# A convolution and low-rank mixer kernel: hand-ordered groups of eight token tiles, tiled matmuls, and transposes by DMA

## The chip, the cores and the metric

The kernel runs on one core of a Trainium2 chip. The metric is device time in microseconds (us). A quoted time is the median of a kernel's runs; a quoted ratio is the mean time of one kernel's fast runs over the mean time of the other's fast runs in the same rounds, so it is not quite the ratio of the two medians.

Engines: PE is TensorE (matmul), PEld its weight loads, DVE is VectorE, ACT ScalarE, POOL GpSimd, SP SyncE. A "tile" of tokens here is 128 tokens; a row or column tile of PE is a part of its 128 by 128 array.

## The reference, cut to what matters

The batch is 8, the sequence 4224 tokens (33 tiles of 128), the model width 192. There are 8 heads of 24 channels and 7 taps; the rank is 32.

```python
# softmax over the 7 taps, then a causal convolution along the sequence, one filter a head
out = np.einsum('hk,bskhg->bshg', w, x_unf)        # -> x of the next part
# mixer
xt = x.transpose(0, 2, 1)
h = xt @ U @ V                                     # U: 4224 x 32, V: 32 x 4224
u = x + h.transpose(0, 2, 1)
ch = np.maximum(u @ w_ch1, 0.0) @ w_ch2            # 192 -> 768 -> 192
return u + ch
```

So there are two large products a token (W1, 192 to 768, and W2, 768 to 192), and a low-rank mix over all tokens of a batch, which needs the whole convolution of that batch first.

## The kernel before

A scheduler chooses the order. For each batch: a convolution as two 128 by 128 band matmuls a head, the product with U over 33 tiles, the product with V, then groups of 4 token tiles (8 groups of 4 and one group of 1), each with PE transposes, W1, ReLU and W2.

```python
for hh in range(H):                                   # conv, 504 or 288 columns
    nc.tensor.matmul(out=cps, lhsT=band_sb[:, hh, :], rhs=x_sb[:, 1+s0:1+s1, hc], start=True,  stop=False)
    nc.tensor.matmul(out=cps, lhsT=pband_sb[:, hh, :], rhs=x_sb[:, s0:s1, hc],    start=False, stop=True)
# ... cut: U and V products on the full array, 192 columns each
for t in range(gt):                                   # two transposes a token tile
    nc.tensor.transpose(out=trps[...], in_=u_sb[:, j, 0:P], identity=ident[:])
    nc.tensor.transpose(out=trps[...], in_=u_sb[:, j, D-P:D], identity=ident[:])
nc.vector.tensor_copy(out=uT_lo, in_=trps[...])       # and uT_hi on ACT
# ... cut: loops over the six 128-wide blocks m of W1, in threes
nc.tensor.matmul(out=h1ps, lhsT=W1_sb[:, m*P:(m+1)*P],   rhs=uT_lo, start=True,  stop=False)
nc.tensor.matmul(out=h1ps, lhsT=W1hp_sb[:, m*P:(m+1)*P], rhs=uT_hi, start=False, stop=True)   # 64 of its rows are zero
# ... cut: ReLU on ACT (two of three) and DVE (one of three), W2, add u, store
```

The width 192 does not fit 128 rows, so the second W1 matmul has 64 rows of zeros: a quarter of the W1 work is spent on them.

The softmax here doesn't subtract the row's maximum and nothing guards it: scores larger than these inputs give would overflow.

## Time and profile before

557.93 us when it was predicted (median of 3 runs).

| | before |
|---|---|
| PE, DVE, ACT busy | 86%, 52%, 45% |
| first W1 matmul starts | 62.3 us |
| PE waits for the band weights | 34.9 us |
| PE waits for the transposed u (uT_lo) | 16.0 us |
| a batch in the steady part | about 62 us |

The first page has these lines: busy time of each engine, then the span in 40 slices in tenths, with the granted PE clock under it.

```profile
PE 481.0 (86%) x3760; PEld 307.3 (55%) x3760; DVE 290.2 (52%) x625; ACT 250.2 (45%) x490; POOL 33.4 (6%) x72
...
PE   0226999999999999999999999999999999978886
...
PEclk9999899999999999999999999999999999989999
DMA  9930912247222921166112911194112011201212
```

PE is at nine tenths or more for nearly all of the span after a slow start, at full clock. The DMA engines are lightly used, save while x loads. The list of waits says what PE stood still for (us in total, times, longest):

```profile
PE cps L208 <- DVE band_sb L167: 34.9, 8, 17.0
PE h1ps L294 <- DVE uT_lo L280: 16.0, 29, 0.8
```

The timeline gives the paces. Here is one group of 4 token tiles on PE (start us, duration us, line, what, count):

```profile
204.06 0.59 PE L303 MATMUL h1ps<-uT_hi,W1hp_sb 128*128 128x512 bf16 x2
204.49 2.38 PE L329 MATMUL smps<-W_sb,rl_sb 128*128 128x192 bf16 x24
206.70 0.22 PE L268 MATMUL trps<-ident,u_sb 128*128 128x128 bf16 x1
206.76 0.22 PE L273 MATMUL trps<-ident,u_sb 128*128 128x128 bf16 x1
...
207.85 0.81 PE L294 MATMUL h1ps<-uT_lo,W_sb 128*128 128x512 bf16 x3 [0.33 <-DVE uT_lo L280]
```

The starts count, not the durations, since matmuls are pipelined: 24 W2 matmuls in 2.21 us (0.092 each), a transpose every 0.056 us, a W1 matmul every 0.215 us.

### The profile page before, as it was taken

How to read it: one execution, taken by the hardware profiler on the slowest of the kernel's cores; microseconds unless marked ns; L12 is line 12 of the kernel's file. 1: busy time of each engine (PE TensorE's matmuls, PEld its weight loads, DVE VectorE, ACT ScalarE, POOL GpSimd, SP SyncE). 2: the span in 40 equal slices, each digit the busy share in tenths (PEclk: the TensorE clock that was granted, in tenths of full speed). 3: DMA queues.
4: the chain of work that ended last, by engine and by line, in shares of the span. 5: the costliest groups of instructions: out<-in, count | busy, mean ns of one | idle time of the engine just before them, and what ended most of it. 6: DMA issues, size and time to landing. Idle time of an engine off the chain costs nothing. (4 is left out here: it accounts for less than half of the span.)

```text
span 558.3 us, 9274 instructions
## 1 busy us (share of the span) xinstructions
PE 481.0 (86%) x3760; PEld 307.3 (55%) x3760; DVE 290.2 (52%) x625; ACT 250.2 (45%) x490; POOL 33.4 (6%) x72
## 2 busy tenths in 40 slices
PE   0226999999999999999999999999999999978886
PEld 0003665666566656666566656665666666645554
DVE  2991754457444844466444844465444744464444
ACT  1113345544555445544554454545444545514443
POOL 9400100010000100010001000010000000000000
PEclk9999899999999999999999999999999999989999
DMA  9930912247222921166112911194112011201212
GB/s 122 159 36 0 117 58 66 75 70 113 77 67 64 117 86 59 58 98 111 58 58 65 146 58 57 58 127 84 58 58 65 28 59 60 78 13 51 64 58 64
DMA packets 75371, 40.69 MB, mean 73 GB/s; under 512 B 41312, under 2 KB 75296, under 8 KB 75296
## 3 DMA queue, kind: packets, MB, share of 16 engines
q0 software_dynamic: 39216, 14.11, 22.3%
q1 hardware_dynamic: 36112, 25.99, 14.8%
q8 instruction: 29, 0.48, 0.4%
q14 instruction: 14, 0.11, 0.1%
HBM read 28.24 MB, written 25.95 MB: 97 GB/s over the span
## 5 line engine op out<-in xcount | busy, mean ns | idle before, releaser
L313 ACT ACTIVATE rl_sb<-h1ps 128x512 bf16<-128x512 f32 (+1 forms) x288 | 152.4, 560 | 75.7 <-PE h1ps L303 68.3
L319 DVE TENSOR_SCALAR rl_sb<-h1ps 128x512 bf16<-128x512 f32 x144 | 92.9, 645 | 153.4 <-PE h1ps L303 71.6
L329 PE MATMUL smps<-W_sb,rl_sb 128*128 128x192 bf16 x1584 | 156.6, 246 | 3.1
L329 PEld LDWEIGHTS <-rl_sb 128*128 128x128 bf16 x1584 | 129.6, 98 | 34.7 <-ACT rl_sb L313 15.7
L222 ACT ACTIVATE y_sb<-cps 128x288 bf16<-128x288 f32 (+1 forms) x128 | 64.1, 501 | 188.4 <-PE cps L215 188.4
L294 PE MATMUL h1ps<-uT_lo,W_sb 128*128 128x512 bf16 (+1 forms) x432 | 123.2, 362 | 19.1 <-DVE uT_lo L280 16.0
L303 PE MATMUL h1ps<-uT_hi,W1hp_sb 128*128 128x512 bf16 (+1 forms) x432 | 124.3, 363 | 0.1
L338 DVE TENSOR_TENSOR out_sb<-smps,u_sb 128x384 f32<-128x384 f32 (+1 forms) x136 | 74.2, 545 | 61.1 <-PE smps L329 59.8
L208 PE MATMUL cps<-x_sb,band_sb 128*128 128x288 bf16 (+1 forms) x128 | 45.3, 354 | 43.3 <-DVE band_sb L167 34.9
L252 DVE TENSOR_TENSOR u_sb<-y_sb,smps 128x384 bf16<-128x384 bf16 (+1 forms) x136 | 68.4, 538 | 8.8 <-PE smps L245 6.2
L294 PEld LDWEIGHTS <-W_sb 128*128 128x128 bf16 x432 | 41.5, 97 | 50.7 <-issue 34.7
L303 PEld LDWEIGHTS <-W1hp_sb 128*128 128x128 bf16 x432 | 41.2, 97 | 46.6 <-issue 12.3
L281 ACT ACTIVATE uT_hi<-trps 128x512 bf16<-128x512 bf16 (+1 forms) x72 | 40.4, 560 | 37.7 <-DVE uT_lo L280 37.1
L215 PE MATMUL cps<-x_sb,pband_sb 128*128 128x288 bf16 (+1 forms) x128 | 45.4, 354 | 1.6 <-DVE pband_sb L185 1.6
L245 PE MATMUL smps<-tt_sb,V_sb 128*128 128x192 bf16 x264 | 43.8, 251 | 2.7 <-DVE u_sb L252 1.3
L268 PE MATMUL trps<-ident,u_sb 128*128 128x128 bf16 x264 | 45.2, 220 | 0.0
L273 PE MATMUL trps<-ident,u_sb 128*128 128x128 bf16 x264 | 45.2, 220 | 0.0
L208 PEld LDWEIGHTS <-band_sb 128*128 128x128 bf16 x128 | 12.6, 98 | 47.8 <-DVE band_sb L167 39.9
L245 PEld LDWEIGHTS <-V_sb 128*128 128x128 bf16 x264 | 25.1, 99 | 24.8 <-issue 7.7
L228 PE MATMUL tt_psum<-y_sb,U_sb 128*32 128x192 bf16 x264 | 30.9, 260 | 4.0 <-ACT y_sb L222 4.0
L273 PEld LDWEIGHTS <-u_sb 128*128 128x128 bf16 x264 | 26.0, 99 | 7.7 <-issue 0.3
L268 PEld LDWEIGHTS <-u_sb 128*128 128x128 bf16 x264 | 26.0, 99 | 6.9 <-issue 0.3
(68 smaller groups left out, 144.9 us busy)
## 6 DMA issues: line engine op xcount, KB each, us to landing
out_dram<-out_sb SPq DMA_DIRECT2D x128, 192.0 KB, 2.0
x_sb<-in_x_dram POOLq DMA_DIRECT2D x8, 1584.0 KB, 13.3
out_dram<-out_sb SPq DMA_DIRECT2D x8, 96.0 KB, 1.6
W_sb<-in_moe_w_ch_dram POOLq DMA_DIRECT2D x1, 288.0 KB, 10.8
U_sb<-in_moe_U_dram POOLq DMA_DIRECT2D x1, 264.0 KB, 14.5
V_sb<-in_moe_V_dram POOLq DMA_DIRECT2D x1, 264.0 KB, 13.5
W_sb<-in_moe_w_ch_dram POOLq DMA_DIRECT2D x1, 192.0 KB, 10.2
W1hp_sb<-in_moe_w_ch_dram POOLq DMA_DIRECT2D x1, 96.0 KB, 9.8
```

The lines of the kernel that those rows point to most:

```text
L208: nc.tensor.matmul(out=cps[:, 0:cb, :], lhsT=band_sb[:, hh, :], rhs=x_sb[:, 1 + s0 : 1 + s1, hc], start=True, stop=False,)
L222: nc.scalar.activation(out=y_sb[:, s0:s1, hc], in_=cps[:, 0:cb, :], func=ACT.Copy)
L245: nc.tensor.matmul(out=smps[:, t, :], lhsT=V_sb[:, j * P : (j + 1) * P], rhs=tt_sb[:], start=True, stop=True,)
L252: nc.vector.tensor_tensor(out=u_sb[:, j0 : j0 + n, :], in0=y_sb[:, j0 : j0 + n, :], in1=smps[:, 0:n, :], op=ALU.add,)
L268: nc.tensor.transpose(out=trps[:, t * P : (t + 1) * P], in_=u_sb[:, j, 0:P], identity=ident[:],)
L273: nc.tensor.transpose(out=trps[:, GT * P + t * P : GT * P + (t + 1) * P], in_=u_sb[:, j, D - P : D], identity=ident[:],)
L294: nc.tensor.matmul(out=h1ps[:, 0:ntok], lhsT=W1_sb[:, m * P : (m + 1) * P], rhs=uT_lo[:, 0:ntok], start=True, stop=False,)
L303: nc.tensor.matmul(out=h1ps[:, 0:ntok], lhsT=W1hp_sb[:, m * P : (m + 1) * P], rhs=uT_hi[:, 0:ntok], start=False, stop=True,)
L313: nc.scalar.activation(out=rl_sb[:, m, 0:ntok], in_=h1ps[:, 0:ntok], func=ACT.Relu,)
L319: nc.vector.tensor_scalar_max(out=rl_sb[:, m, 0:ntok], in0=h1ps[:, 0:ntok], scalar1=0.0)
L329: nc.tensor.matmul(out=chps[:, tt, :], lhsT=rl_sb[:, m, t * P : (t + 1) * P], rhs=W2_sb[:, m, :], start=(m == 0), stop=(m == MC - 1),)
L338: nc.vector.tensor_tensor(out=out_sb[:, 0:n, :], in0=chps[:, 0:n, :], in1=u_sb[:, j : j + n, :], op=ALU.add,)
```

## The change

The intent is to take work off PE and off the start:

- The token tiles of all batches form one row of 264 and are worked in 33 groups of 8, across batch borders, in an order written by hand. W2 of a group runs one group later than its W1.
- W1 has three chunks of 64 rows. The two halves of a group (4 token tiles each) lie on rows 0 to 63 and 64 to 127, so two matmuls of 64 rows can run side by side on two row tiles. No zero rows are left.
- Convolution runs on four 64 by 64 tiles, half the columns.
- The U products use four column tiles of 32, the V products four row tiles of 32. Two small matmuls a batch add up the four partial sums.
- u is transposed by the DMA engines (12 blocks of 128 by 128 a group) instead of PE.
- Band weights come from a strided read of a small DRAM tile instead of 120 DVE operations (so many are in the trace; the prediction says 112); x loads in three chunks.

```diff
-    GT = 4
+    GT = 8
+    NTT = B * NT
+    NG = NTT // GT
+    ctx.enter_context(tc.manual_schedule())
 ...
+    def conv(b, h, i0, i1, engs):
+        for halo in range(2):
+            for r in range(2):
+                for c in range(2):
+                    nc.tensor.matmul(
+                        out=pp[r][HB * c : HB * c + HB, 0 : nn[r] * GS],
+                        lhsT=band[HB * r : HB * r + HB, h, HB * halo : HB * halo + HB],
+                        rhs=xt[b][HB * r : HB * r + HB, st : st + 2 * nn[r] - 1 : 2, hc],
+                        start=(halo == 0), stop=(halo == 1),
+                        tile_position=(HB * r, HB * c),
+                    )
 ...
+            c = ttn[b] % 4                       # U products
+            nc.tensor.matmul(out=ttp[b][32 * c : 32 * c + 32, 0:D], lhsT=U_sb[:, j, :],
+                rhs=yt[b][:, j, :], ..., tile_position=(0, 32 * c))
 ...
+                nc.tensor.matmul(                # V products
+                    lhsT=V_sb[32 * q : 32 * q + 32, (j // 8) * 2 + j % 2, :],
+                    rhs=ttb[b][32 * q : 32 * q + 32, :], ..., tile_position=(32 * q, 0))
 ...
-                nc.tensor.transpose(...)
-            nc.vector.tensor_copy(out=uT_lo[:, 0:ntok], in_=trps[:, 0:ntok])
-            nc.scalar.activation(out=uT_hi[:, 0:ntok], ...)
+        nc.sync.dma_start_transpose(
+            out=uTt[g][:].rearrange("p i c t -> p (i c) t"),
+            in_=ut[g][:].rearrange("p i c f k -> p (i c f k)"))
 ...
+            for c in range(3):                   # W1
+                for hf in range(2):
+                    nc.tensor.matmul(out=pp[hf][:],
+                        lhsT=W1_sb[HB * hf : HB * hf + HB, c, m * P : (m + 1) * P],
+                        rhs=uTt[g][HB * hf : HB * hf + HB, :, c, :],
+                        start=(c == 0), stop=(c == 2), tile_position=(HB * hf, 0))
 ...
+    for g in range(NG + 1):
+        if g + 1 < NG:
+            h_group(g + 1)
+            transp(g + 1)
+        for b in loadq.get(g, []):               # x of a later batch, all chunks at once
+            x_tile(b)
+            for ch in XCH:
+                x_load(b, *ch)
+        if g < NG:
+            w1(g)
+        for b, h in convq.get(g, []):
+            conv(b, h, 0, NB1, "AA")
+        ...                                      # W2 of group g - 1, U products
```

## The prediction

> **What bounds it now.** PE, in order. The first page shows PE 86% busy, DVE 52%, ACT 45%. Start-up takes 62 us to the first W1 matmul; in it PE waits 34.9 us for the DVE that builds the bands (list of waits). After that PE is at nine tenths or more per slice, granted clock near 1.0. The timeline gives the paces: 512-column W1 matmuls start every 0.215 us, 192-column W2 matmuls every 0.092 us (24 in 2.21 us), transposes every 0.056, 504-column conv matmuls every 0.21, U and V products 0.083 to 0.1. Per batch (estimate): W1 21.3, W2 18.2, conv 5.4, U and V products 6.3, transposes 3.7: 55 us, against about 62 measured; the rest is waits (PE on uT_lo 16 us in all, on conv evictions 11).
>
> **What the change does, on PE.** Per group of 8 tiles (33 groups, no ragged ninth):
> - W1: 36 matmuls of 512 columns and 64 rows, in pairs on two row tiles. The Trainium skill, "TensorEngine Tiling (Array Packing)", Tiling Modes, says tiles run in parallel; no trace of before shows it. If pairs overlap: 18 x 0.215 = 3.9 us instead of 5.2.
> - W2 unchanged: 48 x 0.092 = 4.4 us.
> - V products on four 32-row tiles, U products on four 32-column tiles: 0.4 us at best instead of 1.5; 1.2 if weight loads bind.
> - conv on four 64x64 tiles: half the columns, 0.7 us instead of 1.3.
> - transposes off PE (0.9 us), their evictions off DVE and ACT (28 and 40 us in all).
> - added: two sum matmuls a batch, four mode switches a group, which the skill says drain the array: I allow 0.5 to 1 us with bank waits.
>
> Estimate 10.3 us a group, against about 15. 33 x 10.3 = 340 us.
>
> **Start and end.** Bands come from a strided DRAM round trip instead of 112 DVE operations; x arrives in three chunks, conv follows. W1 should start at about 28 us, limited by x (13 us landing) and then V and W1 loads. End: last W2 plus store, 7 us. Sum 375 us; I add 10 for DMA trouble.
>
> **Other engines.** Per group ACT: 8 ReLUs x 0.6 + conv 1.7 = 6.5 us; DVE: 4 x 0.69 + adds 4.5 = 7.3 us. DMA: stores 2.5, x 3.8 (83 and 124 us of 16 engines now, over 33), plus a 0.39 MB transpose: at the 261 GB/s of the skill's "DMA: Bandwidth & Descriptors", Latency and other measured facts, 1.5 us (estimate); at the 51 ns a packet that x shows, 1536 pieces on 16 engines take 4.9 us (estimate), and DMA at 11 us a group is even with PE.
>
> **Predicted:** 385 us, 8 in 10 between 350 and 435; faster 0.94, same 0.03, slower 0.03.
>
> **What would show it.** Right: W1 matmuls start 0.11 us apart; conv 0.04 to 0.05; V products under 0.05; ACT and DVE under 75%; first W1 before 30 us; group period 10 to 11 us; PE rarely waiting on uT. Wrong: W1 starts still 0.215 apart (then near 500 us); PE waits on uT by DMA, longest while x loads (shared engines): a transpose landing over about 8 us after issue costs its excess each group; PE waits for banks behind ACT at the start of each W1 block; granted clock well below 1.
>
> **What would make it wrong.** Row-tile pairs that do not overlap; transposes over 10 us each; DMA saturation; larger drains; one eight-bank PSUM pool in strict order stalling PE behind ReLUs.

## The result, and the profile after

The changed kernel takes 393.02 us (median of 4 runs), the one before 558.93 us in the same rounds: ratio 0.7033, with a 95% interval of 0.7006 to 0.706. The results are correct. The forecast of 385 us, with a range of 350 to 435, holds the measured time, but several of its terms were off and cancelled, so the terms have to be looked at one by one.

First page of the changed kernel:

```profile
PE 330.9 (84%) x3956; PEld 221.1 (56%) x3956; DVE 236.6 (60%) x485; ACT 189.1 (48%) x410; POOL 46.2 (12%) x77
...
PE   0070599969996999969996999959999999999995
...
PEclk9996599999999899989999899978999999999998
DMA  9999925993599456994599456992544574546524
```

PE still bounds the steady part, but after the start there are now five slices at five or six tenths, about one batch apart, and next to them the granted clock falls. The list of waits of PE:

```profile
PE ps L311 <- DMA uT<-u_sb: 32.2, 6, 12.8
...
PE ps L183 <- DMA band<-g_dr: 19.9, 2, 19.3
```

L311 is the W1 matmul. The timeline shows an undisturbed group and then one of the waits:

```profile
159.14 4.06 PE L311 MATMUL ps<-uT,W_sb 64*128 64x512 bf16 x36
163.12 0.88 PE L183 MATMUL ps<-x_sb,band 64*64 64x384 bf16 x16
163.94 4.13 PE L333 MATMUL ps<-W_sb,rl_sb 128*128 128x192 bf16 x48
168.01 0.34 PE L256 MATMUL ps<-tt_sb,V_sb 32*128 32x192 bf16 x8
171.51 5.75 PE L311 MATMUL ps<-uT,W_sb 64*128 64x512 bf16 x36 [3.16 <-DMA uT<-u_sb]
```

Three things are to be seen. The 36 W1 matmuls take 4.06 us, so two do run side by side. PE then waits 3.16 us for the transposed u. And the W1 block after that wait takes 5.75 us instead of 4.06. The clock records of the trace have the reason: 3.4 us at half clock just after that wait. Of the five steady waits (3.31, 3.75, 3.16, 4.41 and 4.78 us, 19.4 us in all), four bring half clock for 3.4 or 6.8 us, which begins near the wait's end. The Trainium skill, "TensorE: Matmul & The Clock Gate", Part 1, says that PE's clock is halved after a window of about 3.4 us without work. The trace agrees on the length, but not every such window was empty. All changes of the clock in this trace lie on one grid of 3.413 us (half clock begins at 127.82, 172.19, 216.57 and 260.94 us, each 13 x 3.413 us after the one before). Three times the grid window just before was wholly idle; before 172.19 us it was not, since W1 had already run for its last 0.7 us. The wait of 3.31 us (81.7 to 85.0 us) was cut in two by a border of the grid at 83.45 us, and brought no half clock: where a wait falls counts as well as how long it is. The longer W1 blocks cost another 7.5 us (the excess of four blocks over 4.06 us).

The queues show what else went on. POOL began to issue a later batch's x at 153 us, and the transpose was issued at 160.86, while x was still landing:

```profile
153.50 0.75 POOL L76 DMA_DIRECT2D x_sb<-in_x_dram  x1 [0.28 <-issue]
...
160.86 3.01 SPq L297 DMA_TRANSPOSE uT<-u_sb  x1
```

It landed 10.6 us after issue. For all transposes of the run:

```profile
DMA to landing us min/median/max: 3.6/4.1/12.7
```

In the five steady collisions, landing time less PE's wait is 7.2 to 7.6 us. That is the slack of a group: a transpose that lands within it costs nothing.

The start is the other surprise (first waits of 12.8 us on uT and 19.3 us on the band):

```profile
19.28 0.33 PE L183 MATMUL ps<-x_sb,band 64*64 64x144 bf16 x2 [19.28 <-DMA band<-g_dr]
...
43.31 7.01 PE L311 MATMUL ps<-uT,W_sb 64*128 64x512 bf16 x36 [12.76 <-DMA uT<-u_sb]
```

The first W1 starts at 43.3 us, where 28 had been forecast.

### The profile page after: what moved, and what is told of

It reads as the page before. It is cut to its first block, busy times and chain, and to the rows that moved or that the text cites. A ratio compares the mean times of both kernels' runs of the same rounds, so it can differ in the third digit from the quotient of the medians.

```text
span 393.3 us, 9471 instructions
## 1 busy us (share of the span) xinstructions
PE 330.9 (84%) x3956; PEld 221.1 (56%) x3956; DVE 236.6 (60%) x485; ACT 189.1 (48%) x410; POOL 46.2 (12%) x77
## 2 busy tenths in 40 slices
DMA packets 130044, 54.63 MB, mean 139 GB/s; under 512 B 95248, under 2 KB 129936, under 8 KB 130000
## 3 DMA queue, kind: packets, MB, share of 16 engines
q1 hardware_dynamic: 88864, 39.41, 44.6%
## 4 chain that ended last, share of the span: by engine, by line
PE 71%; DMA 22%; DVE 3%; ACT 1%; issue 0%; SPq 0%; DVEq 0%
PE ps L311 34%; PE ps L333 28%; DMA uT<-u_sb 17%; PE ps L183 5%; DMA band<-g_dr 2%; PE ps L256 2%; PE ps L210 2%; DMA g_dr<-g_sb 1%; DVE out_sb L341 1%; ACT y_sb L196 1%; DMA out_dram<-out_sb 1%; DMA w_sb<-in_weight_dram 1%; DVE tt_sb L233 1%; DVE u_sb L278 0%; DVE g_sb L142 0%
## 5 line engine op out<-in xcount | busy, mean ns | idle before, releaser
L321 ACT ACTIVATE rl_sb<-ps 128x512 bf16<-128x512 f32 x264 | 134.8, 619 | 160.9 <-PE ps L311 129.8
L311 PE MATMUL ps<-uT,W_sb 64*128 64x512 bf16 x1188 | 148.9, 398 | 32.3 <-DMA uT<-u_sb 32.2
L333 PE MATMUL ps<-W_sb,rl_sb 128*128 128x192 bf16 x1584 | 137.5, 246 | 0.0
L311 PEld LDWEIGHTS <-W_sb 64*128 64x128 bf16 x1188 | 63.5, 98 | 107.8 <-issue 34.7
L341 DVE TENSOR_TENSOR out_sb<-ps,u_sb 128x384 f32<-128x384 f32 x132 | 73.5, 558 | 78.2 <-PE ps L333 77.1
L323 DVE TENSOR_SCALAR rl_sb<-ps 128x512 bf16<-128x512 f32 x132 | 88.3, 690 | 48.2 <-PE ps L311 48.1
L278 DVE TENSOR_TENSOR u_sb<-y_sb,ps 128x192 bf16<-128x192 bf16 (+1 forms) x168 | 66.3, 461 | 0.6 <-PE ps L256 0.6
L196 ACT ACTIVATE y_sb<-ps 128x384 bf16<-128x384 f32 (+3 forms) x136 | 53.5, 516 | 18.7 <-PE ps L183 18.5
L183 PE MATMUL ps<-x_sb,band 64*64 64x408 bf16 (+4 forms) x640 | 30.6, 319 | 20.0 <-DMA band<-g_dr 19.9
L81 POOL DMA_DIRECT2D x_sb<-in_x_dram x24 | 18.8, 785 | 0.4
L76 POOL DMA_DIRECT2D x_sb<-in_x_dram x24 | 18.1, 754 | 1.8 <-issue 1.8
L256 PEld LDWEIGHTS <-V_sb 32*128 32x128 bf16 x264 | 4.6, 92 | 10.3 <-issue 10.3
```

Source lines behind the costliest of these rows:

```text
L76: nc.gpsimd.dma_start(out=xt[b][0:HB, 1 + i0 : 1 + e0, :], in_=x[b, i0 * HB : e0 * HB, :].rearrange("(j p) d -> p j d", p=HB),)
L81: nc.gpsimd.dma_start(out=xt[b][HB:P, s0 : i1 + 1, :], in_=x[b, (NB0 - 1 + s0) * HB : (NB0 + i1) * HB, :].rearrange("(j p) d -> p j d", p=HB),
L183: nc.tensor.matmul(out=pp[r][HB * c : HB * c + HB, 0 : nn[r] * GS], lhsT=band[HB * r : HB * r + HB, h, HB * halo : HB * halo + HB], rhs=xt ...
L196: nc.scalar.activation(out=o, in_=i, func=ACT.Copy)
L256: nc.tensor.matmul(out=banks[pr][:, a * D : (a + 1) * D], lhsT=V_sb[32 * q : 32 * q + 32, (j // 8) * 2 + j % 2, :], rhs=ttb[b][32 * q : 32 ...
L278: nc.vector.tensor_tensor(out=u_group(g)[:, i : i + n, :, hf, :], in0=yt[b][:, run[0] : run[0] + n, :].rearrange("p n (c k) -> p n c k", c=3),
```

## The experiments

Theory A: a transpose is late because x loads share the DMA engines with it, and PE loses the wait plus a cold clock. Rival B: it is late by its own length, or because it stands behind the stores in its queue. Further runs test what the tiles themselves are worth, and what holds up the start. In each, all of the changed kernel is kept except for the edit shown (cut to its main lines). No run takes out conv's four tiles, the later W2 or the hand-written order alone, so what each of these is worth is not shown.

### No x loads after the first two batches (wrong result)

```diff
         for b in loadq.get(g, []):
-            x_tile(b)
-            for ch in XCH:
-                x_load(b, *ch)
+            xt[b] = xt[b - 2]
```

> Wrong result on purpose: batches 2 to 7 reuse the x tiles of batches 0 and 1, so no x is loaded after the first groups. Theory A (transposes land late because x loads share the 16 DMA engines): every transpose lands about 4 us after issue, PE waits on uT only at the start (about 10 us instead of 32.2), the granted clock stays at 1.0 after the first group, time 360 to 368 us. Theory B (a transpose is late by its own length or by standing behind the stores in its queue): waits and time stay within 4 us of the changed kernel's 393.

Measured: 360.72 us, ratio to before 0.6455. As meant, the result is wrong. PE's waits on uT:

```profile
PE ps L311 <- DMA uT<-u_sb: 5.9, 1, 5.9
```

All five steady waits are gone and the slowest transpose landed in 5.3 us; the stores in the transposes' queue are unchanged. B falls: the loss comes with the x loads. The first W1 also starts earlier, at 35.5 us. The 32.3 us gained agree in size with 19.4 us of waits, 7.5 us of half clock and 7.8 us at the start (34.7 in sum).

### The same x loads, spread and placed after a transpose

```diff
-    xs = ctx.enter_context(tc.tile_pool(name="xs", bufs=2))
+    xs = ctx.enter_context(tc.tile_pool(name="xs", bufs=3))
 ...
-        loadq.setdefault(max(1, G - 10), []).append(b)
+        for n, ch in enumerate(XCH):
+            loadq.setdefault(G - 8 + n, []).append((b, ch))
 ...
-        for b in loadq.get(g, []):
-            x_tile(b)
-            for ch in XCH:
-                x_load(b, *ch)
+        for b, ch in loadq.get(g, []):
+            nc.gpsimd.tensor_copy(out=gate[:], in_=uTt[g + 1][:, 0, 0, 0:2])   # POOL waits for the transpose
+            if xt[b] is None:
+                x_tile(b)
+            x_load(b, *ch)
```

> Three x buffers, and each third of a batch's x is issued only after a group's transpose has landed. Theory A: as many bytes as in the changed kernel, yet PE waits on uT fall below 14 us and the time to 360 to 370 us. Theory B: unchanged, 389 to 394. If x lateness matters instead (conv waits for x), PE waits on x appear at conv and the time stays above 380.

Measured: 371.11 us as the median of all four runs; one, 378.98 us, counts as slow, and the three fast ones have a median of 369.85 us. Ratio (fast runs alone) 0.6632, correct. The bytes are the same, 54.63 MB, and yet:

```profile
PE ps L312 <- DMA uT<-u_sb: 7.1, 3, 5.7
...
PE ps L184 <- DMA x_sb<-in_x_dram: 3.3, 4, 1.0
...
DMA to landing us min/median/max: 3.6/4.7/7.9
```

So it is not the volume that costs, but a transpose that meets more of x than it has slack for. The meeting itself is not gone: beside a third of x, transposes still land in up to 7.9 us, about the slack of a group, and the steady waits on uT shrink to 1.4 us. The time is at the upper edge of the expected range: x now sometimes lands just after conv wants it (3.3 us in 4 waits).

### The transposes back on PE

```diff
-        nc.sync.dma_start_transpose(...)
+        for half in range(2):                      # placed after W1 and conv of the group before
+            pb = psp.tile([P, 6 * P], BF16, name="ps", tag="ps")
+            for n in range(6):
+                nc.tensor.transpose(out=pb[:, n * P : (n + 1) * P], in_=..., identity=ident[:])
+            # first half evicted by ACT, second by DVE
```

> Transposes back on PE (12 per group at 0.056 us, evicted once by ACT and once by DVE), all else of the change kept. Theory A: PE gains 0.67 us a group plus a mode switch, 22 to 27 us in all, and loses the 20 us of uT waits, 9 us of half clock and 8 us at the start: 370 to 385 us, so the DMA transpose gained nothing. Rival (taking transposes and their evictions off PE, ACT and DVE is a main part of the gain): 405 us or more.

Measured: 378.99 us, ratio 0.6774, correct. As written, the DMA transpose is a loss of 14 us. Against the spread version it is a gain of 8 us: the DMA transpose pays as long as no whole batch of x loads beside it; thirds of a batch left it its gain. Twelve transposes start over 0.67 us a group, 22 us in all (estimate, 33 groups), and a single wait of PE on uT is left:

```profile
PE ps L333 <- DVE uT L320: 0.4, 1, 0.4
```

### W1 on all 128 rows

```diff
-    W1_sb = cst.tile([P, 3, M4], BF16, name="W1_sb")
+    W1_sb = cst.tile([P, 2, 3, M4], BF16, name="W1_sb")     # zeros in the other half's rows
 ...
-                        lhsT=W1_sb[HB * hf : HB * hf + HB, c, m * P : (m + 1) * P],
-                        rhs=uTt[g][HB * hf : HB * hf + HB, :, c, :],
-                        tile_position=(HB * hf, 0),
+                        lhsT=W1_sb[:, hf, c, m * P : (m + 1) * P],
+                        rhs=uTt[g][:, :, c, :],
```

> W1 with the same 36 matmuls of 512 columns a group, but on all 128 rows with zeros in the other half of the weights, so no two can run at once. If the row-tile pairs really run side by side: 36 x 0.215 = 7.7 us a group instead of 4.04, and 33 x 3.7 us less some 20 to 30 us of waits hidden behind it: 485 to 500 us. Rival (W1 blocks are held by ReLU evictions, ACT 4.03 us a group, not by matmuls): under 430 us.

Measured: 488.97 us, ratio 0.8737, correct. The number, the columns and the order of the matmuls are those of the changed kernel; each now has 128 rows, half of them zeros, and the second tile is gone:

```profile
202.11 7.94 PE L313 MATMUL ps<-uT,W_sb 128*128 128x512 bf16 x36
209.99 0.88 PE L185 MATMUL ps<-x_sb,band 64*64 64x384 bf16 x16
```

7.94 us against 4.06: the row tiles run side by side, at very nearly twice the pace. With W1 that long the steady waits on uT vanish too (only the first, 12.6 us, is left), so the 96 us added are less than 33 x 3.88 = 128. Against the scheme before (24 matmuls of 0.215 us for 8 tiles, 5.2 us) the pair is worth 1.1 us a group.

### The order of the W1 matmuls

```diff
-            for c in range(3):
-                for hf in range(2):
+            for hf in range(2):
+                for c in range(3):
```

> The W1 loop runs three matmuls on one half of the rows, then three on the other, instead of alternating. If matmuls start in program order and only neighbours on different row tiles overlap, four matmul lengths pass per six matmuls instead of three: 5.2 us a group instead of 4.04, 37 us in all less some 10 us of waits absorbed: 418 to 432 us. If PE reorders freely, 393; if such an order gives no overlap at all, about 490.

Measured: 392.73 us, ratio 0.7016: no change, against the expectation. The block of 36 still takes 4.07 us. At the start of a block, the start times in the trace (us; this table is not a view of the profile) come in pairs:

```
changed kernel   deltas of starts: 0.004 0.222 0.003 0.213 0.003 0.213 0.003 ...
three by three   deltas of starts: 0.010 0.216 0.010 0.206 0.010 0.206 0.010 ...
```

Three matmuls for one row tile stand in the program before the first for the other, and still two start within 10 ns of each other. (Later in some blocks the second of a pair starts 30 to 60 ns after the first, in both kernels; the period stays 0.216 us.) The semaphore marks in the trace fit: in all 31 blocks looked at, both matmuls of the first pair carry a wait and both of the third report a finished sum, so a pair is one matmul of each half. The compiler did not undo the edit: when this run's kernel.py is built again, the compiled instructions stand three and three. A matmul on one row tile does not wait for an earlier one on another row tile. How PE does it is not shown; that the order inside six matmuls does not matter here is.

### U and V products on one tile

```diff
-            c = ttn[b] % 4
+            c = 0
 ...
-                    lhsT=V_sb[32 * q : 32 * q + 32, (j // 8) * 2 + j % 2, :],
-                    rhs=ttb[b][32 * q : 32 * q + 32, :],
-                    tile_position=(32 * q, 0),
+                    lhsT=V_sb[0:32, j, :],
+                    rhs=ttb[b][0:32, :],
+                    tile_position=(0, 0),
```

Not shown: V is now loaded once, onto 32 rows, instead of in four parts, and the two sum matmuls use 32 rows.

> U products all on one 32-column tile and V products all on one 32-row tile, nothing else changed. If the tiles run side by side in the changed kernel (33 U products in 0.92 us, 8 V products in 0.34 us there), they now take about 3.3 us a batch and 0.7 us a group: 8 x 2.4 + 33 x 0.35 = 31 us more, less up to 10 us that waits for transposes absorb: 413 to 424 us. Rival (the pace of these products came from the new order, not from tiles): 393 to 397 us.

Measured: 395.53 us, ratio 0.7079. The products are slower as expected, yet the time hardly moves:

```profile
157.01 2.90 PE L198 MATMUL ps<-y_sb,U_sb 128*32 128x192 bf16 x33
...
172.28 0.83 PE L246 MATMUL ps<-tt_sb,V_sb 32*128 32x192 bf16 x8
```

They take 2.90 us and 0.83 us, against 0.92 and 0.34 on four tiles. But the waits on uT fell from 32.2 to 10.8 us (the first one is nearly all of that) and the mean clock rose from 0.953 to 0.98, with no half clock left in the steady part. The sum closes: 8 x 1.98 and 33 x 0.49 us are 32 us more of products, less 21.4 us of waits and 7.5 us of half clock, which leaves 3.1 us; 2.5 were measured. The slower U products stand between the issue of x and the issue of the next transpose: POOL starts on x at 155.1 us here and the transpose is issued at 164.9, so it comes 2 us later into the load than in the changed kernel, and a longer group gives it more time. The work was not hidden, it took the place of waits. To test that, the same edit was made in the final kernel (below), which has no such waits:

> The one-tile U and V products again, now in the kernel without waits for transposes (359.7 us). In the changed kernel they added about 4 us of PE work a batch, yet only 2 us in all; the theory is that waits for transposes, which lasted as long, took it up. If so nothing takes it up here: 8 x 2 + 33 x 0.49 = 32 us more, and some 4 us for V in one load of 32 partitions: 388 to 397 us. If the PE work was hidden by something else, 362 to 368 us.

Measured: 386.71 us against 359.67 us there: 27 us more, where the changed kernel lost 2.5. That is just under the expected 388 to 397; PE idled 2.3% between 100 and 340 us in the final kernel and 0.8% in this one between 100 and 350, so some of it still went into idle time. About 6.6 of the 27 us fall before the first W1 (39.5 us against 32.9), and part of these may come from the other way of loading V: conv too starts 2.5 us later. The saving of the tiles is real, and in the changed kernel it was given back as waiting.

### The start: three attempts

The band weights go to DRAM and back while x loads: 5.8 us for the write and 8.1 for the reads to land. Two runs put the rest of x, U, V and W behind the band, one after a third of x, one after two thirds. A third holds batch 1's x back until the first transpose has landed.

```diff
     x_load(0, *XCH[0])
+    # the band's code moved up to here in band_first (after XCH[1] in band_mid)
+    nc.gpsimd.tensor_copy(out=gate[:], in_=band[:, 0, 0:2])
     x_load(0, *XCH[1])
 ...
     transp(0)
+    nc.gpsimd.tensor_copy(out=gate[:], in_=uTt[0][:, 0, 0, 0:2])    # gate_x1 alone
     x_tile(1)
 ...
-        slots = [1] * 4 + [2] * 4 if b == 1 else ...
+        slots = [2] * 8 if b == 1 else ...                              # gate_x1 alone
```

> Only the first third of x is issued before the band weights have landed; the rest of x, U, V and W wait for them. If the band's trip through DRAM is slow because it shares the DMA with x (5.9 us for the write, 8.2 us for the read in the changed kernel), the band lands by 12 us instead of 20, the first W1 starts by 39 us instead of 43.3 and the time is 386 to 390 us. Rival (the start is bound by the volume of x and weights, which now comes later): first W1 at 43 us or later, 393 us or more.

> As the run before it, but two thirds of x go ahead of the band. Contention theory: band by about 14 us, first W1 at 36 to 39 us, 385 to 389 us. Volume rival: no change, 391 to 395 us.

> The load of batch 1's x waits until the first transpose has landed; batch 1's conv moves from groups 1 and 2 to group 2. Contention theory: the first transpose lands about 4 us after issue instead of 10.8, the first W1 starts at 37 to 38 us; the second and third transposes then meet the load instead, so the gain in time is anything from 5 us to none: 387 to 394 us.

Measured: 394.9 (ratio 0.7081), 395.6 (0.7083) and 398.26 us (0.7152), all correct, none better than 393. In the first, the band's DMAs are as quick as hoped (2.6 and 3.0 us) and conv starts at 11.0 us instead of 19.3, but then U is late, and the wait reappears further on:

```profile
PE ps L311 <- DMA uT<-u_sb: 34.0, 6, 13.9
PE ps L183 <- DMA band<-g_dr: 11.4, 2, 11.0
PE ps L210 <- DMA U_sb<-in_moe_U_dram: 7.0, 1, 7.0
```

The first W1 starts at 43.7 us: what ends the start is the first transpose, which lands amid the loads of batches 1 and 2, and an earlier band does not touch that. The second run goes the same way (first conv at 14.3 us, first transpose landed at 44.5, first W1 at 44.7). Both give the rival's numbers, though not for the rival's reason. Holding batch 1 back brings the first W1 to 37.4 us, as expected, but the next transposes then meet the same load (30.2 us of waits in 7 places, the first of them 5.2), and the time is 4 us above the expected range. The meeting was moved, not avoided. A combination of the spread loads (one group earlier), the band after two thirds of x, and the gate:

> Spread x loads one group earlier than in the spread run, with the band after two thirds of x and the gated batch 1. If the parts add up: 371 less 3 us of x waits at conv less 5 to 9 us of start: 358 to 364 us; correct result. If the start is volume-bound: 368 us or more.

Measured: 371.53 us, ratio 0.666, correct: no better than the spread loads alone (0.6632). The parts do not add up, for the same reason: a wait of 5.45 us on a transpose ends at 57.3 us. The earlier band moves the first W1 by 0.5 us only, from 37.4 us with the gate alone to 36.9, and U is late here as well (4.9 us). What an earlier band would bring in the final kernel below was not run.

### A version that beats both kernels

What was left is a place where x must load whatever one does, the first three groups. There the transposes go back to PE; later groups use the DMA, with spread loads.

```diff
+    NPE = 3
 ...
+        if g >= NPE:                       # transpose by DMA, else the PE version shown above
+            nc.sync.dma_start_transpose(...)
 ...
+            loadq.setdefault(max(0, G - 9 + n), []).append((b, ch))   # spread as above, one group earlier
```

> The spread x loads, one group earlier from batch 3 on, and PE transposes for the first three groups alone, where x of batches 1 and 2 must load anyway. Theory A (what is left of the loss is transposes meeting x at the start): first W1 at about 34 us at full clock, hardly any wait on uT, 360 to 367 us, correct. Rival (spread loads leave other waits): 368 us or more.

Measured: 359.67 us (359.13 to 361.12, four runs), ratio to before 0.6438 with a 95% interval of 0.6415 to 0.6461, correct. This is just under the expected range. Over the changed kernel's ratio of 0.7033 that is 8.5% less (each ratio is to the kernel before, on its own chip).

```profile
PE   0086999999999999999999999999999999999995
...
PEclk9998999999999999999999999999999999999999
DMA  9999598599959898699949996699934555655525
...
PE ps L341 <- DMA uT<-u_sb: 1.6, 2, 1.0
...
32.88 5.41 PE L341 MATMUL ps<-uT,W_sb 64*128 64x512 bf16 x36 [0.42 <-DVE uT L328]
```

The first W1 starts at 32.9 us and the waits on uT are 1.6 us. It is as fast as the run without x loads, while it loads all of x.

## Why the prediction was right or wrong

The sum was right (385 forecast, 393 measured), and so was the direction and what bounds the kernel. Three of its terms were off, in both directions, so the nearness of the sum (8 us) is luck in part; that the pairs of W1 run side by side as forecast is not.

- **"W1 should start at about 28 us": wrong, 43.3 us.** The failed step is "limited by x (13 us landing), then V and W1 loads". The first W1 waits 12.8 us for the first transpose, which lands among x loads of the next two batches that the forecast had not placed in time. The band's trip was slow as well (first conv at 19.3 us), but making it quick gained nothing. The run with PE transposes for the first groups, where the first W1 starts at 32.9 us, shows that the transpose was what could be removed. The term was too small by 15 us: 7.8 us went with batch 2's x in the run without later loads (first W1 at 35.5 us), 2.6 more with the PE transposes (32.9 us), and the last 4.9 no run took away.
- **"Estimate 10.3 us a group": mis-sized.** From the first W1 (43.3 us) to the start of the last group's W2 (384.5 us; the forecast counts this W2 with the end) the 33 groups take 341 us, 10.3 each, but that is a coincidence of two errors. An undisturbed group with conv takes 9.2 us (W1 starts at 304.08 and again at 313.28 us); all groups together, without the 27 us of waits and half clock of the next point, take 314 us, 9.5 each. One part is W2: I took 0.092 us, the mean pace of before. There the median distance of two W2 starts is 0.083 us; the mean is higher since W2 directly follows its ReLUs and sometimes waits for them (one start in the group shown above comes 0.31 us after the one before; W2's weight loads wait 15.7 us in all for ReLUs on ACT). The change puts W2 one group behind, and all 48 run at 0.083: 4.0 us instead of 4.4. The rest lies in the terms given as ranges: 10.3 less 3.9, 4.4 and 0.7 leaves 1.3 us for the U and V products, switches and bank waits together, and these came to less (see below).

```profile
304.08 4.11 PE L311 MATMUL ps<-uT,W_sb 64*128 64x512 bf16 x36
308.12 0.89 PE L183 MATMUL ps<-x_sb,band 64*64 64x384 bf16 x16
308.94 4.13 PE L333 MATMUL ps<-W_sb,rl_sb 128*128 128x192 bf16 x48
313.00 0.34 PE L256 MATMUL ps<-tt_sb,V_sb 32*128 32x192 bf16 x8
313.28 4.11 PE L311 MATMUL ps<-uT,W_sb 64*128 64x512 bf16 x36
```

- **"PE rarely waiting on uT" against "longest while x loads (shared engines)".** The second held. The five steady waits and the half clock after four of them cost 27 us, where I had added 10 for "DMA trouble". The mechanism was named, its size was not: a colliding transpose lands 10.5 us or more after issue, where the median is 4.1, and half clock was named only as a sign, without a cost. The threshold given, "over about 8 us after issue costs its excess", was nearly right: the slack is 7.2 to 7.6 us.
- **"If pairs overlap: 18 x 0.215 = 3.9 us": right.** 4.06 us measured, 7.94 us without the second tile.
- **"V products 0.4 us at best ... 1.2 if weight loads bind": nearly the best case.** 0.34 us a group for V, and 0.92 us a batch for U, 0.22 us a group. But in this kernel that saving was given back as waiting: taking it away cost only 2.5 us here, and 27 us where nothing waits.
- **"conv ... 0.7 us": right.** 16 matmuls in 0.88 us, two heads a group in 24 of the 33 groups and four in two more.
- **"four mode switches a group ... 0.5 to 1 us with bank waits": just under its lower end.** A switch lengthens the distance of two starts by about 0.1 us (0.178 us from W2 to V, against 0.083 inside W2 and 0.082 from W2 to the sum matmuls, which also use the full array), so four are 0.4 us (estimate).
- **"ACT and DVE under 75%": right**, 48% and 60%.
- **DMA, "a 0.39 MB transpose ... 1.5 us ... 4.9 us (estimates)": in between.** The queue that carries stores and transposes was busy for 44.6% of 393 us after and 14.8% of 558 us before, on 16 engines; the difference over 33 is 2.8 us a transpose (estimate, which also holds the small band transfers). The volume did not bind: the same bytes, spread out, cost no steady waits worth naming.

Added up: 28 became 43.3 (+15.3), 33 groups became 341 instead of 340, the end 9 instead of 7, and the 10 us allowance is spent inside the 341: 385 - 10 + 18.3 is 393.

## What to carry to other kernels

A shared transfer engine should be planned like a shared compute engine: before moving a step from PE to DMA, write down what else the DMA moves in the group in which the step's result is needed, and place large loads after the latency-critical transfer, in pieces small enough for its slack, with a further buffer if need be. A saving on the bounding engine is worth its size only if no wait stands ready to take it; test a part by removing it in a version that has no such waits, else a real gain looks like nothing. And when a forecast comes out right, check its terms: here the start was 15 us longer, the groups 26 us shorter (33 x (9.5 - 10.3)) and the waits 17 us more than allowed (27 - 10), which left 8 us of error with the end.

## What the Trainium skill lacked or had wrong

- "TensorE: Matmul & The Clock Gate", Part 3, says that matmuls are strictly first in, first out in start and end, without reordering. With three W1 matmuls on one row tile ahead of three on the other, starts still came in pairs, one of each tile, every 0.216 us (10 ns apart at the start of a block), and the 36 took 4.07 us as in the alternating order. Across row tiles the statement does not hold here.
- "TensorEngine Tiling (Array Packing)", Key Properties, says that a change of tiling mode drains TensorE, but gives no cost. In the changed kernel a switch adds about 0.1 us between two starts (0.178 us against 0.083).
- "DMA: Bandwidth & Descriptors", Latency and other measured facts, gives 261 GB/s for a DMA transpose, or 350 to 400 for the contiguous case. Here 0.39 MB took at best 3.6 us from issue to landing, which is 109 GB/s with all fixed costs in it, 10.5 to 12.7 us when it met a whole batch of x, and up to 7.9 us beside a third of one. No page that I used gives a transpose's latency beside other loads.
- The halved clock after an idle window, of "TensorE: Matmul & The Clock Gate", Part 1, agreed in length: four of five waits of 3.2 to 4.8 us brought 3.4 or 6.8 us of half clock, on a grid of 3.413 us. But the window needs no full idleness: before 172.19 us PE had worked for 0.7 of its 3.4 us, and the clock was halved all the same. The 3.31 us wait that ended at 85 us lay across two windows and brought none.
